# Which wait a reload leaves behind, and the order of two inverse mixings, in a gated convolution and MLP kernel

## The chip, the cores and the metric

The kernel runs on one core of a Trainium2 chip. Its time is the device time of one execution in microseconds (us); a median of several executions is quoted. Five engines run their own instruction streams and meet through semaphores: TensorE (PE in the profile; matmuls), VectorE (DVE; elementwise work), ScalarE (ACT; here it empties PSUM), GpSimd (POOL; here it issues accumulating DMA transfers) and SyncE (SP; issues the other transfers). A ratio is the mean time of one kernel's fast runs over that of the kernel before in the same rounds on the same chip, so it is not quite the ratio of the medians that stand beside it. Brackets after a ratio are its 95% interval.

## The reference, cut to what matters

```python
g = sigmoid((q * gate_w).sum(-1, keepdims=True))
kv = shift_conv4(k) * v                               # S = 2048 rows, D = 640 columns
y  = irfft(rfft(pad(kv)) * rfft(pad(ssm_k)))[:S]      # long convolution along S
a  = q * (y + kv * ssm_D)
b  = mlp_over_S(layernorm(q))                         # S -> 1536, gelu, -> S
return g * a + (1 - g) * b
```

The four-row phases p = 0..3 of the sequence are transformed as matmuls and combined by elementwise "mixing" steps, in both directions. The inverse is made in two halves of the output rows.

## The kernel before: the parts concerned

Every operation is handed to a small list scheduler in the program, which works out an order for each engine from dependencies and assumed durations, and then to a tracker, which emits the semaphore waits.

```python
# tracker: emits a DMA. "wait" is an extra region that must be complete first.
def dma(self, stream, out_ap, in_ap, semname, ..., wait=()):
    reads = [in_ap] + ([out_ap] if accum else []) + list(wait)   # recorded as read by the DMA
    acc = self.pre(stream, reads, [out_ap])                      # waits
    ...
    for reg, mode in acc:
        self.add_record(reg, mode, ("dma", semname, v))          # later writers wait for this DMA
# scheduler side of the same helper
    rd = [i] + ([o] if accum else []) + list(kw.get("wait", ()))

def invmix(Ya, Yb, sc, z0, z2):    # eight VectorE steps of 128 x 2560
    S0 = a0 + a1;  a0 = a0 - a1    # m1, m2
    S1 = b0 + b1;  b0 = b0 - b1    # m3, m4 (m4 overwrites b0)
    a1 = S0 + S1;  b1 = S0 - S1    # m5 -> inverse tile p=0, m6 -> p=2
    oA = ...;      oB = ...        # m7 -> p=1, m8 -> p=3
# ... (written out from the tensor_tensor calls)

chained(product, A0[1], ...)       # last spectral product with an accumulating DMA: C1 += SS ("C<-SS")
for kt in range(2):                # q_hi is scratch until that sum is done; now reload it with q
    dma(q_hi[:, kt], q_from_HBM, 128 * 5120, wait=[H(A0[1], 1)])
chained(product, A0[0], ...)
for kt in range(2):
    dma(q_lo[:, kt], q_from_HBM, 128 * 5120).after.add(w2last)
Z0 = invmix(A0[0], A0[1], C3a, None, None);      inverse(0, Z0)   # m1..m8
Z1 = invmix(A1[0], A1[1], (SS, 0), None, None);  inverse(1, Z1)   # n1..n8
```

m1 to m8 are the first half's steps, n1 to n8 the second half's. For each tile p, 16 matmuls make the inverse, ScalarE scales two results into cgb, and VectorE multiplies by q ("q product").

Of the kernel before, what the change touches and what calls it, by code (L numbers as in the profile page):

```python
# [13 lines left out]
ALU = mybir.AluOpType  # L14
# [4 lines left out]
class _Tracker:  # L19
# [231 lines left out]
        self.dma_cnt[name] = 0  # L251

    def dma(self, stream, out_ap, in_ap, semname, transpose=False, noncontig=False, accum=False, wait=()):
        reads = [in_ap] + ([out_ap] if accum else []) + list(wait)
        writes = [out_ap]
        acc = self.pre(stream, reads, writes)
        engobj = self.eng[stream]
        sem = self.dma_sems[semname]
        if transpose:
            ins = engobj.dma_start_transpose(out_ap, in_ap)  # L260
        elif accum:
            ins = engobj.dma_start(out_ap, in_ap, accum_op=ALU.add, max_dma_last_dim=2560)  # L262
        elif noncontig:
            with self.nc.allow_non_contiguous_dma(reason="tiny"):
                ins = engobj.dma_start(out_ap, in_ap)
        else:
            ins = engobj.dma_start(out_ap, in_ap)
        ins.then_inc(sem, 16)
        self.dma_cnt[semname] += 16
        v = self.dma_cnt[semname]  # L270
        self.dma_hist[(semname, v)] = dict(self.known[stream])
        src = ("dma", semname, v)
        for reg, mode in acc:
            self.add_record(reg, mode, src)
        return v
# [234 lines left out]
def _build(nc, A_q, A_k, A_v, A_shift_k, A_ssm_k, A_ssm_D, B_x, B_w1, B_b1, B_w2, B_b2, gate_w, out):  # L510
    Bsz, S, D = A_q.shape
# [9 lines left out]
    with ExitStack() as es:  # L521
# [8 lines left out]
        SC = _Sched(T, pp)  # L530
# [4 lines left out]
        def alloc(name, shape, dtype, at=None):  # L535
            size = mybir.dt.size(dtype)
            for s_ in shape[1:]:
                size *= s_
            if at is None:
                off = cur[0]  # L540
                cur[0] = (off + size + 63) // 64 * 64
            else:
                off = at
            assert off % 4 == 0 and off + size <= top, f"SBUF overflow {name}: {off}+{size} > {top}"
            h = nc.alloc_sbuf_tensor_at(name, list(shape), dtype, offset=off)
            T.reg_sbuf(h, off)
            return h

        def base_of(h):
            return T.mem[h.name][1]  # L550

        def V(h, off, dims, p0=0, pn=128):
            row = T.mem[h.name][2]
            return bass.AP(tensor=h, offset=p0 * row + off, ap=[[row, pn]] + [list(d) for d in dims])
# [26 lines left out]
        SS = alloc("SS", [128, 2, 4, D], BF16)  # L581
# [22 lines left out]
        q_hi = alloc("q_hi", [128, 2, 4, D], BF16, at=base_of(Drow))  # L604
# [3 lines left out]
        def n_of(ap):  # L608
            n = 1
            for st, ct in [tuple(p) for p in ap.ap][1:]:  # L610
                n *= ct
            return n

        def dve_dur(n, mode):
            return n / {1: 960.0, 2: 1920.0, 4: 3840.0}[mode] + (0.04 if mode == 4 else 0.08)
# [4 lines left out]
        def tt(eng, o, a, b, op, mode=2, prio=None, xr=()):  # L620
            n = n_of(o)
            d = dve_dur(n, mode) if eng == "DVE" else n / 600.0 + 0.17
            rd = [a, b] + list(xr)
            o_ = SC.add(eng, d, lambda s: T.op(eng, lambda e: e.tensor_tensor(o, a, b, op), rd, [o]),  # L624
                        rd, [o], prio=prio, name="tt")
            o_.lock = True
            return o_
# [23 lines left out]
        def act(o, i, func, bias=None, scale=None, acc=None, vt=None, prio=None, name="act"):  # L651
            kw = {}
            rr = []
            nap = 0
            for k_, v_ in (("bias", bias), ("scale", scale)):
                if v_ is not None:
                    kw[k_] = v_
                    if isinstance(v_, bass.AP):
                        rr.append(v_)
                        nap += 1  # L660
            ww = [o]
            if acc is not None:
                kw["accum_out"] = acc
                ww.append(acc)

            def emit(s):
                src = i(s) if vt is not None else i
                return T.op("ACT", lambda e: e.activation(o, src, func, **kw), rr + [src], ww)  # L668
            return SC.add("ACT", act_dur(n_of(o), nap), emit, rr if vt is not None else rr + [i], ww, prio=prio, vt=vt, name=name)
# [31 lines left out]
        def dma(o, i, nbytes, stream="SP", prio=None, sem=None, rate=365.0, chain=False, **kw):  # L701
            if sem is None:
                sem = f"d{ndma[0]}"
                ndma[0] += 1
            if sem not in T.dma_sems:
                T.add_dma_sem(sem, es.enter_context(nc.semaphore(f"s_{sem}")))
            rd = [i] + ([o] if kw.get("accum") else []) + list(kw.get("wait", ()))
            o_ = SC.add(stream, nbytes / rate / 1000.0, lambda s: T.dma({"QA": "ACT"}.get(stream, stream), o, i, sem, **kw), rd, [o], prio=prio, lat=-1.0, name="dma")
            if chain:
                if last[0] is not None:  # L710
                    o_.after.add(last[0])
                last[0] = o_
            return o_

        def dr(t, off, ap):
            return bass.AP(tensor=t.tensor, offset=t.offset + off, ap=ap)
# [383 lines left out]
        for n_, hk in enumerate(HORD):  # L1100
            for a in range(3):
                w2last = dma(W2[:, W2S[n_][a]:W2S[n_][a] + 4, :], dr(B_w2, a * 4 * 128 * S + 512 * hk, [[S, 128], [128 * S, 4], [1, 512]]), 128 * 4096)
            for p in range(4):
# [13 lines left out]
                if not last_:  # L1117
                    o_ = act(O1[:, hk, p, :].rearrange("p (a b) -> p a b", a=2), two, ACT.Identity, bias=c2[:, t:t + 1], scale=omg[:, t:t + 1], vt=vt, name="o1")

        A0 = {0: (C[2], 2), 1: (C[1], 0)}  # L1120
        A1 = {0: (C[3], 2), 1: (C[3], 0)}
# [9 lines left out]
        def H(hs, c):  # L1131
            h, s = hs
            return V(h, s * SL + 1280 * c, [[SL, 2], [1, 1280]])
# [24 lines left out]
        C3a = (C[2], 0)  # L1158

        def acc_dma(dst, src):  # L1160
            (hd, sd), (hs, ss) = dst, src
            for i in range(2):
                o = V(hd, (sd + i) * SL, [[1280, 2], [1, 1280]])
                i_ = V(hs, (ss + i) * SL, [[1280, 2], [1, 1280]])
                dma(o, i_, 128 * 5120, stream="POOL", prio=0, accum=True)
# [22 lines left out]
                dma(comp(V1[g], i, 0), tmp, 128 * 5120, stream="POOL", prio=0, accum=True)  # L1188


        def invmix(Ya, Yb, sc, z0, z2):
            def sl(h, s):
                return V(h, s * SL, [[1, SL]])

            def pr(h, s, rev=False):
                return V(h, s * SL + (1280 if rev else 0), [[-1280 if rev else 1280, 2], [1, 1280]])
            (ha, sa), (hb, sb), (hs, ss) = Ya, Yb, sc
            tt("DVE", sl(hs, ss), sl(ha, sa), sl(ha, sa + 1), ALU.add)
            tt("DVE", sl(ha, sa), sl(ha, sa), sl(ha, sa + 1), ALU.subtract)
            tt("DVE", sl(hs, ss + 1), sl(hb, sb), sl(hb, sb + 1), ALU.add)  # L1200
            tt("DVE", sl(hb, sb), sl(hb, sb), sl(hb, sb + 1), ALU.subtract)
            tt("DVE", sl(ha, sa + 1), sl(hs, ss), sl(hs, ss + 1), ALU.add)
            tt("DVE", sl(hb, sb + 1), sl(hs, ss), sl(hs, ss + 1), ALU.subtract)
            oA = V(hs, ss * SL, [[SL + 1280, 2], [1, 1280]])
            oB = V(hs, (ss + 1) * SL, [[-1280, 2], [1, 1280]])
            tt("DVE", oA, pr(ha, sa), pr(hb, sb, True), ALU.add)
            tt("DVE", oB, pr(ha, sa), pr(hb, sb, True), ALU.subtract)
            return {0: (ha, sa + 1), 2: (hb, sb + 1), 1: (hs, ss), 3: (hs, ss + 1)}

        def inverse(h, Z):  # L1210
# [40 lines left out]
        def chained(f, *a):  # L1251
            n0 = len(SC.ops)
            f(*a)
            new = [o for o in SC.ops[n0:] if o.eng == "DVE"]
            for o in new:
                o.after.update(lastp[-1:])
            lastp.append(new[-1])
# [4 lines left out]
        acc_dma(A1[1], V1[1])  # L1262
        acc_dma(A1[0], V1[0])
        chained(product, A0[1], A0[1], V0[1], H(V0[1], 0))
        for kt in range(2):
            dma(q_hi[:, kt, :, :], dr(A_q, 512 * kt * D, [[4 * D, 128], [1, 4 * D]]), 128 * 5120, wait=[H(A0[1], 1)])
        chained(product, A0[0], A0[0], V0[0])
        for kt in range(2):
            dma(q_lo[:, kt, :, :], dr(A_q, (1024 + 512 * kt) * D, [[4 * D, 128], [1, 4 * D]]), 128 * 5120).after.add(w2last)
        Z0 = invmix(A0[0], A0[1], C3a, None, None)  # L1270
        inverse(0, Z0)
        Z1 = invmix(A1[0], A1[1], (SS, 0), None, None)
        inverse(1, Z1)

        SC.run()
# [35 lines left out]
```

## Time and profile before

| | before |
|---|---|
| first three executions | 183.45, 184.76, 185.66 us; median 184.76 |
| span of the profiled execution (first to last instruction) | 181.9 us |
| TensorE busy, VectorE busy | 173.2 us, 171.3 us |
| TensorE's idle time from 100 us to its last matmul | 1.74 us, one hole before 158.25 |

The span is what the profile shows; the device time is some 2 us more.

### The profile page before, as it was taken

The page shows a single profiled execution, that of the slowest core. Times are in us where ns is not written, and L with a number is a line of the kernel's source. Part 1 is how long each engine was busy: PE and PEld are TensorE (multiplying, and loading weights), DVE is VectorE, ACT ScalarE, POOL GpSimd, SP SyncE. Part 2 cuts the span into 40 slices and gives each one's busy share as a digit, 9 for nine tenths or more (in the row PEclk, how much of TensorE's full clock was granted, in tenths as well). Part 3 has the DMA queues.
Part 4 walks back from the last instruction along what each step waited for, and adds up shares of the span by engine and source line. Part 5 has one row for each costly group of instructions (what it writes and reads, how often), then busy time and mean ns, then how long its engine had stood idle before and what let it go on. Part 6 is the DMA issues. An engine that isn't in the chain of part 4 may idle for free.

```text
span 181.9 us, 3336 instructions
## 1 busy us (share of the span) xinstructions
PE 173.2 (95%) x1380; PEld 129.3 (71%) x1381; DVE 171.3 (94%) x203; ACT 116.9 (64%) x176; POOL 45.3 (25%) x42
## 2 busy tenths in 40 slices
PE   7969998899999999999999999999999999699993
PEld 2636785586778677776777778888888887477772
DVE  7999895999999999999999899999999996999974
ACT  5798998899898999428999911322313225156760
POOL 4089404580000055000241101205252000041300
PEclk9999999999999999999999999999999999999999
DMA  5999999999999999998499799797999999146787
GB/s 159 376 410 370 389 269 200 266 397 300 213 262 269 176 279 234 230 229 220 110 269 260 147 180 349 143 216 236 189 194 227 204 241 416 66 76 144 123 258 271
DMA packets 38542, 43.51 MB, mean 239 GB/s; under 512 B 15867, under 2 KB 31360, under 8 KB 38528
## 3 DMA queue, kind: packets, MB, share of 16 engines
q1 hardware_dynamic: 33296, 32.16, 58.0%
q0 software_dynamic: 5200, 11.14, 35.2%
q8 instruction: 11, 0.18, 0.4%
q14 instruction: 3, 0.02, 0.0%
q10 hardware_dynamic: 32, 0.01, 0.0%
HBM read 25.87 MB, written 2.62 MB: 157 GB/s over the span
## 4 chain that ended last, share of the span: by engine, by line
PE 47%; ACT 19%; DVE 18%; DMA 11%; issue 3%; SPq 0%; DVEq 0%
PE pp L293 47%; DVE C L624 10%; DMA C<-SS 5%; DMA q_hi<-in_A_q_dram 5%; ACT C L668 5%; ACT gq L668 5%; DVE tm L624 4%; ACT FTB L668 3%; ACT wT L668 3%; DVE q_hi L624 2%; ACT ksh L668 2%; ACT GT L668 2%; DVE SS L624 1%; ACT L668 1%; DVE O L680 0%
## 5 line engine op out<-in xcount | busy, mean ns | idle before, releaser
L293 PE MATMUL pp<-X,ring 128*128 128x320 bf16 x384 | 55.4, 299 | 0.0
L624 DVE TENSOR_TENSOR C<-C 128x2560 bf16<-128x2560 bf16 (+2 forms) x37 | 54.5, 1521 | 0.3 <-DMA q_hi<-in_A_q_dram 0.3
L293 PE MATMUL pp<-GT,W 128*128 128x320 bf16 x384 | 52.8, 299 | 0.0
L293 PEld LDWEIGHTS pp<-GT,W 128*128 128x128 bf16 x384 | 43.5, 113 | 8.7
L293 PEld LDWEIGHTS pp<-X,ring 128*128 128x128 bf16 x384 | 37.4, 98 | 14.4
L668 ACT ACTIVATE C<-pp 128x640 bf16<-128x640 f32 x64 | 40.4, 724 | 4.7 <-PE pp L293 4.7
L668 ACT ACTIVATE O<-pp,c,omg 128x640 bf16<-128x640 f32 x15 | 13.2, 883 | 33.8 <-PE pp L293 33.8
L262 POOL DMA_DIRECT2D C<-C x8 | 10.9, 1610 | 41.9 <-DVE C L624 38.4
L293 PE MATMUL pp<-wT,FTB 128*128 128x320 bf16 x112 | 17.2, 299 | 2.6 <-ACT wT L668 1.5
L668 ACT ACTIVATE cgb<-pp,gg 128x640 bf16<-128x640 f32 x16 | 12.7, 793 | 8.5 <-PE pp L293 8.5
L293 PEld LDWEIGHTS pp<-wT,FTB 128*128 128x128 bf16 x112 | 10.5, 98 | 7.9 <-ACT wT L668 2.0
L668 ACT ACTIVATE GT<-pp,cc 128x640 bf16<-128x640 f32 x12 | 9.5, 795 | 9.0 <-PE pp L293 9.0
L293 PE MATMUL pp<-C,FTB 128*128 128x320 bf16 x96 | 13.5, 299 | 1.7 <-DVE C L624 1.7
L624 DVE TENSOR_TENSOR tm<-C,C 128x2560 bf16<-128x2560 bf16 (+1 forms) x7 | 14.3, 2057 | 0.0
L920 DVE BATCH_NORM_STATS2 stats<-X 128x6 f32<-128x320 bf16 x32 | 13.5, 462 | 0.0
L293 PEld LDWEIGHTS pp<-C,FTB 128*128 128x128 bf16 x96 | 9.3, 98 | 5.6 <-issue 2.0
L624 DVE TENSOR_TENSOR SS<-C 128x2560 bf16<-128x2560 bf16 x8 | 11.8, 1486 | 1.3 <-DMA C<-C 1.3
L262 POOL DMA_DIRECT2D C<-q_hi x6 | 5.9, 977 | 27.7 <-DVE C L624 13.2
L262 POOL DMA_DIRECT2D O<-q_hi x4 | 4.8, 1200 | 28.5 <-DVE q_hi L624 28.5
L668 ACT ACTIVATE gq<-gq 128x640 bf16<-128x640 bf16 x16 | 11.8, 739 | 0.0
L624 DVE TENSOR_TENSOR C<-tm 128x2560 bf16<-128x2560 bf16 (+1 forms) x9 | 10.6, 1191 | 0.1
L668 ACT ACTIVATE wT<-pp 128x1024 bf16<-128x1024 f32 x10 | 9.7, 1043 | 1.0 <-PE pp L293 1.0
(73 smaller groups left out, 200.4 us busy)
## 6 DMA issues: line engine op xcount, KB each, us to landing
ring<-in_B_w_dram SPq DMA_DIRECT2D x12, 512.0 KB, 9.9
W<-in_B_w_dram SPq DMA_DIRECT2D x12, 512.0 KB, 6.3
C<-C POOLq DMA_DIRECT2D x8, 640.0 KB, 10.5
X<-in_A_q_dram SPq DMA_DIRECT2D x4, 640.0 KB, 8.4
kn<-in_A_k_dram SPq DMA_DIRECT2D x4, 640.0 KB, 9.1
out_dram<-O SPq DMA_DIRECT2D x7, 320.0 KB, 3.0
C<-SS POOLq DMA_DIRECT2D x3, 640.0 KB, 11.5
ssm<-in_A_ssm_k_dram SPq DMA_DIRECT2D x3, 512.0 KB, 6.8
```

Source lines behind the costliest of these rows:

```text
L262: ins = engobj.dma_start(out_ap, in_ap, accum_op=ALU.add, max_dma_last_dim=2560)
L293: ins = self.nc.tensor.matmul(ps_ap, lhsT=lhsT, rhs=rhs, start=start, stop=stop, skip_group_check=True)
L624: o_ = SC.add(eng, d, lambda s: T.op(eng, lambda e: e.tensor_tensor(o, a, b, op), rd, [o]), rd, [o], prio=prio, name="tt")
L668: return T.op("ACT", lambda e: e.activation(o, src, func, **kw), rr + [src], ww)
L920: ops.append(SC.add("DVE", 0.38, (lambda o, i: lambda s: T.op("DVE", lambda e: e.bn_stats(o, i), [i], [o]))(o, i), [i], [o]))
```

## The change

Its intent: the reload of q_hi has to wait for the last sum C<-SS, but nothing that overwrites C1 afterwards has to wait for the reload; and the second half's mixing shall not be put in front of the first half's, since the first half's tiles are needed first.

```diff
     def dma(self, stream, out_ap, in_ap, semname, ..., wait=()):
-        reads = [in_ap] + ([out_ap] if accum else []) + list(wait)
+        reads = [in_ap] + ([out_ap] if accum else [])
         writes = [out_ap]
+        if wait:
+            self.pre(stream, list(wait), [])
         acc = self.pre(stream, reads, writes)
...
-            rd = [i] + ([o] if kw.get("accum") else []) + list(kw.get("wait", ()))
+            rd = [i] + ([o] if kw.get("accum") else [])
...
+            for o_ in SC.ops[n0:]:          # at the end of invmix
+                o_.after.update(behind or ())
...
+        lastacc = SC.ops[-1]
...
-            dma(q_hi[...], ..., wait=[H(A0[1], 1)])
+            dma(q_hi[...], ..., wait=[H(A0[1], 1)]).deps.add(lastacc)
...
-        Z0 = invmix(A0[0], A0[1], C3a, None, None)
+        Z0 = invmix(A0[0], A0[1], C3a)
+        z0last = SC.ops[-1]
         inverse(0, Z0)
-        Z1 = invmix(A1[0], A1[1], (SS, 0), None, None)
+        Z1 = invmix(A1[0], A1[1], (SS, 0), False, [z0last])
```

(An option to start the mixing with b is added too and not used.) I call the first half of it, the record of the reload, part 1, and the order of n behind m part 2.

More of the change, by code (lines that the diff above doesn't have):

```diff
@@ L1188, in cross, with invmix @@
                 dma(comp(V1[g], i, 0), tmp, 128 * 5120, stream="POOL", prio=0, accum=True)
-        def invmix(Ya, Yb, sc, z0, z2):
+        def invmix(Ya, Yb, sc, bfirst=False, behind=None):
+            n0 = len(SC.ops)
             def sl(h, s):
@@ L1197, in invmix @@
             (ha, sa), (hb, sb), (hs, ss) = Ya, Yb, sc
-            tt("DVE", sl(hs, ss), sl(ha, sa), sl(ha, sa + 1), ALU.add)
-            tt("DVE", sl(ha, sa), sl(ha, sa), sl(ha, sa + 1), ALU.subtract)
-            tt("DVE", sl(hs, ss + 1), sl(hb, sb), sl(hb, sb + 1), ALU.add)
-            tt("DVE", sl(hb, sb), sl(hb, sb), sl(hb, sb + 1), ALU.subtract)
+            for (hy, sy), k in (((hb, sb), 1), ((ha, sa), 0)) if bfirst else (((ha, sa), 0), ((hb, sb), 1)):
+                tt("DVE", sl(hs, ss + k), sl(hy, sy), sl(hy, sy + 1), ALU.add)
+                tt("DVE", sl(hy, sy), sl(hy, sy), sl(hy, sy + 1), ALU.subtract)
             tt("DVE", sl(ha, sa + 1), sl(hs, ss), sl(hs, ss + 1), ALU.add)
@@ L1264, in _build @@
         chained(product, A0[1], A0[1], V0[1], H(V0[1], 0))
+        lastacc = SC.ops[-1]
+        assert lastacc.eng == "POOL"
         for kt in range(2):
-            dma(q_hi[:, kt, :, :], dr(A_q, 512 * kt * D, [[4 * D, 128], [1, 4 * D]]), 128 * 5120, wait=[H(A0[1], 1)])
+            dma(q_hi[:, kt, :, :], dr(A_q, 512 * kt * D, [[4 * D, 128], [1, 4 * D]]), 128 * 5120, wait=[H(A0[1], 1)]).deps.add(lastacc)
         chained(product, A0[0], A0[0], V0[0])
```

## The prediction

> **What bounds the kernel now.** I read the page first: TensorE is busy 173.2 us and VectorE 171.3 us of a span of 181.9, so two engines are nearly full and only a wait that ends in an empty TensorE can be worth anything. The chain of work that ended last, in order of time, says where such a wait may be. Its end in the kernel before:
>
> ```profile
> 133.98 9.76 DMA C<-SS
> ...
> 144.19 9.53 DMA q_hi<-in_A_q_dram
> ...
> 153.81 4.31 DVE C L624 x3
> 158.12 0.14 issue
> 158.25 20.82 PE pp L293 x152
> 179.08 0.02 issue
> 179.10 0.55 DVE O L680
> ```
>
> Columns are start, duration, engine or transfer, what it writes. Read upwards: the last 20.8 us are unbroken matmuls; they were released by three VectorE operations; those by the reload of q_hi from HBM (the diff's title says "key", the loads are of A_q); and that by the accumulating transfer C<-SS, the last addition to the second spectrum of the first half. A serial chain of two transfers, 133.98 to 153.72, stands in front of the inverse mixing.
>
> The chain overstates its worth: while the transfers ran, TensorE had other work. So I next read TensorE alone in order of time:
>
> ```profile
> 142.77 8.31 PE L293 MATMUL pp<-GT,W 128*128 128x320 bf16 x60
> 150.92 2.34 PE L293 MATMUL pp<-C,FTB 128*128 128x320 bf16 x16
> 153.10 3.42 PE L293 MATMUL pp<-GT,W 128*128 128x320 bf16 x24
> 158.25 2.33 PE L293 MATMUL pp<-C,FTB 128*128 128x320 bf16 x16 [1.74 <-DVE C L624]
> 160.43 2.34 PE L293 MATMUL pp<-GT,W 128*128 128x320 bf16 x16
> ```
>
> C,FTB is the inverse transform, GT,W the second matmul of the MLP, used as filler. There is one hole, 1.74 us before 158.25, and none elsewhere from 100 us on: the table of waits from there to the end has this as the only wait of TensorE. VectorE in the same stretch:
>
> ```profile
> 143.64 4.30 DVE L624 TENSOR_TENSOR C<-C 128x2560 bf16<-128x2560 bf16 x3
> 147.85 1.49 DVE L624 TENSOR_TENSOR SS<-C 128x2560 bf16<-128x2560 bf16 x1
> 149.25 1.48 DVE L624 TENSOR_TENSOR C<-C 128x2560 bf16<-128x2560 bf16 x1
> 152.01 1.49 DVE L624 TENSOR_TENSOR SS<-C 128x2560 bf16<-128x2560 bf16 x1 [1.28 <-DMA C<-C]
> 153.81 4.30 DVE L624 TENSOR_TENSOR C<-C 128x2560 bf16<-128x2560 bf16 x3 [0.30 <-DMA q_hi<-in_A_q_dram]
> 158.02 0.82 DVE L624 TENSOR_TENSOR q_hi<-cgb,q_hi 128x1280 bf16<-128x1280 bf16 x1
> ```
>
> Call the eight steps of the first half's inverse mixing m1 to m8, those of the second half n1 to n8 (in the order of the new source: add a, subtract a, add b, subtract b, then the four outputs 5, 6, 7, 8 that feed inverse tiles p = 0, 2, 1, 3). From the output names and the order in which the program's own scheduler issues the kernel before, the rows are m1, m3, m2; n3; m5; n1; m4, n2, m6; then the first q product. So m4 is the step held by q_hi, m6 comes two steps behind it, and p2 cannot run before m6 ends at 158.11. The n1 in front of m4 waited 1.28 us for the second half's last C<-C accumulation. The source explains m4: the reload records the "wait" region as read by the transfer itself, so m4, which overwrites C1[0], has a write-after-read wait on the reload's landing, though the reload reads HBM.
>
> **What the Trainium skill says.** "DMA: Bandwidth & Descriptors", section "Rules for kernel authors", says that an accumulating transfer must have signalled before another access of the same bytes; so the wait of the mixing on C<-SS is a true one and must stay. Here it landed at 143.74, and m3 needs it from 145.0: no cost left. Its section "Anatomy of one DMA" gives 2.0 us plus bytes over 436 GB/s, which would be an estimate of 3.5 us for a 640 KB reload; the trace has 9.53, since four reloads and the accumulations overlap, and the trace decides. "VectorE: DVE Perf Modes", section "The perf-mode tier table", caps tensor_tensor in bf16 at 2x: 2560 / 1.92 GHz = 1.33 us; the trace steps by 1.40 from start to start. "TensorE: Matmul & The Clock Gate", section "Wait — 56ns, not 53.3ns?", gives N / 2.4 GHz + 2.5 ns, 135.8 ns at 320 columns; the trace has 20.81 us for 152 matmuls, 136.9 ns, at granted clock 1.00. So no engine can go faster; only the hole can go.
>
> **The change, part by part.**
> Part 1, the reload's wait on the last sum only: the same wait is issued on the same queue, and the explicit dependency keeps its place in the schedule. The reload still starts at 143.8 and lands at about 153.7. Removed is m4's wait on it. No instruction is added or removed.
>
> Part 2, n1 to n8 behind m8: removed are the two second-half steps (n3, n1) in front of m4 and n2 in front of m6, and with n1 its 1.28 us wait, since C<-C has landed (152.0) long before n1 runs.
>
> I replay VectorE with 1.40 us a step of 2560, 0.74 for a q product, and 0.1 where a step needs the one before it. m1, m3, m2: 143.64 to 147.85 as now. m4 takes the place of n3: to 149.25. m5: to 150.65, as now, so p0 starts on TensorE at 150.92, as now. m6: to 152.05. m7: to 153.55. m8: to 154.97. q product p0 to 155.71: its q_hi landed at 153.7 and its p0 tile left PSUM at 154.09 (as in the trace, 153.30 + 0.79), so neither stops it. n1 to 157.1, q product p2 to 157.9, n2 to 159.3, q product p1 to 160.0, n3 to 161.4, q product p3 to 162.1, n4 to 163.5, n5 to about 165.0.
>
> TensorE: a tile p is 16 matmuls, 2.19 us. p0 150.92 to 153.11; p2 (needs m6, 152.05) to 155.30; p1 (m7, 153.55) to 157.49; p3 (m8, 154.97) to 159.68. The filler left is 24 + 16 = 40 matmuls, 5.48 us: to 165.16. Then n5 is due: 165.0 plus about 0.15 for the signal, so a gap of 0 to 0.1. The second half's 64 inverse matmuls take 8.76, the last 24 of the MLP 3.29: end at 177.2 to 177.3. Check by the sum: 192 matmuls from 150.92 are 26.28 us, 177.20. Before it was 179.06 to 179.08. The gain is 1.85 (the hole with its signal), less up to 0.1: about 1.75 us.
>
> VectorE agrees: after m5 it has 11 steps of 1.40 and 4 products of 0.74, 18.4 us, in both kernels. Before it took 150.73 to 170.78, 20.05 us, of which 1.28 + 0.30 were idle. The last n8 now ends near 169.2, and p3 of the second half needs it only at 171.7. The tail (last scale-and-add 0.55, store to 181.9) hangs on the last matmul as before and is unchanged. So 1.75 / 181.9 = 0.95%: the median 184.76 becomes 183.0.
>
> The change looks larger on the chain than it is: it takes about 10 us of transfer off it, and most of that goes to nothing because TensorE filled the time with MLP matmuls that must be done anyway.
>
> **Rivals.**
> 1. The hole moves rather than closes. Four first-half tiles now run back to back, and the filler that was spread between p0 and p1 must cover until n5. My replay leaves 0 to 0.1 us, with nothing in hand. If VectorE loses 1 us between 150 and 165 (say, the first q product waiting for a late q_hi: slack 154.97 - 153.72 = 1.25), the hole is back at p0 of the second half. That would give 183.9 to 184.8. For it: no margin. Against: every VectorE time in it is from this trace, and the C<-C wait is gone.
> 2. The scheduler, seeing the gap before n5, uses the last MLP tile (24 matmuls, kept in PSUM for the final additions) as filler. Then the kernel would end on an inverse tile and its tail: after TensorE's end, evacuation to +1.0 (as for p0), product 0.82, add 0.49, scalar 0.38, two scale-and-adds 1.2, about 3.9 instead of 0.55. At most some 3 us worse than my time: 185 to 186. Against: this tile has the lowest priority and 40 others stand before it; with the scheduler's own constants (1.0875 us per eight matmuls, 1.41 a step) my hand replay has n5 ready less than 0.1 us before the filler ends. Close, but it holds.
> 3. Nothing: the true wait is on C<-SS, and the reload was hidden anyway. Against: m4 shows the reload's landing as its releaser (0.30), and removing only that would move it by 0.30; but part 2 removes n3, n1 and n2 from in front too. That would be the size (some 0.3 us) if reordering failed: 184.5.
> 4. More than 1.75 us: the timed runs of before spread from 183.45 to 185.66, and its profiled run, at 183.71, lies low in them. If slower runs are those with a later landing of the reload, they carry a bigger hole, and the new kernel, with 1.25 us of slack, would save up to 1 us more: 182.
>
> **Range and chances.** The time is 183.0. The range 181.6 to 184.5 takes in rivals 3 and 4 at its ends and the spread of the runs (about 0.6% either way). Faster by over 2% needs 3.7 us, twice the only hole that exists: 0.03. Slower by over 2% needs rival 2 with bad luck on top: 0.02. Within 2%: 0.95.
>
> **What would show it.** Right: in the changed profile VectorE runs eight mixing steps of the first half without idle from 143.6 to about 155, the next step, SS<-C, has no wait on C<-C, TensorE shows four inverse tiles in a row (64 matmuls on C from 150.9), then 40 MLP matmuls, and no wait above 0.3 us; the last matmul ends near 177.3. The chain no longer contains q_hi. Wrong: a TensorE wait on SS or C near 165 (rival 1), GT,W matmuls not the last on TensorE (rival 2), or p0 starting later than 150.9 because C<-SS landed later.

## The result, and the profile after

The changed kernel took 181.81 us (median of 6; 181.63 to 182.82), the kernel before in the six executions by then 183.76; ratio 0.988 [0.9832, 0.9927]. That is faster by 1.2%, inside 2%. The chain that ended last, in order of time, in the changed kernel (start, duration, what):

```profile
37.59 3.29 ACT ksh L670 x4
40.89 0.05 issue
40.93 136.12 PE pp L295 x1048
177.06 0.02 issue
177.08 0.55 DVE O L682
```

The transfers have left the chain. From 40.93 us to the last scale-and-add it is one unbroken run of 1048 matmuls. TensorE in order of time:

```profile
150.68 8.86 PE L295 MATMUL pp<-C,FTB 128*128 128x320 bf16 x64
159.37 5.60 PE L295 MATMUL pp<-GT,W 128*128 128x320 bf16 x40
164.93 4.51 PE L295 MATMUL pp<-C,FTB 128*128 128x320 bf16 x32
169.27 4.51 PE L295 MATMUL pp<-SS,FTB 128*128 128x320 bf16 x32
173.62 3.42 PE L295 MATMUL pp<-GT,W 128*128 128x320 bf16 x24
```

The four inverse tiles of the first half stand together (64), the 40 filler matmuls behind them, and no line carries a wait in brackets. VectorE over the same stretch:

```profile
143.40 8.50 DVE L626 TENSOR_TENSOR C<-C 128x2560 bf16<-128x2560 bf16 x6
151.94 2.89 DVE L626 TENSOR_TENSOR C<-C,C 128x2560 bf16<-128x2560 bf16 x2
154.75 0.82 DVE L626 TENSOR_TENSOR q_hi<-cgb,q_hi 128x1280 bf16<-128x1280 bf16 x1
155.49 1.48 DVE L626 TENSOR_TENSOR SS<-C 128x2560 bf16<-128x2560 bf16 x1
```

m1 to m8 run without a break from 143.40, the first q product follows at 154.75, and n1 (SS<-C) finds its accumulation landed: no bracket either. VectorE's waits of 1.28 and 0.30 us are gone.

**Where the 2.2 us of span went.** The two profiles also differ before the change matters: p0 starts at 150.92 in one and at 150.68 in the other, although the instructions up to there are the same. From the start of p0 to the start of the two last scale-and-adds it is 178.43 - 150.92 = 27.51 us before and 176.41 - 150.68 = 25.73 after: 1.78 us is the hole. The other 0.24 is the start, and about 0.2 the last store. The experiments say which of this is real.

### The profile page after: what moved, and what is told of

It reads as the page before. It is cut to its first block, busy times and chain, and to the rows that moved or that the text cites. A ratio compares the mean times of both kernels' runs of the same rounds, so it can differ in the third digit from the quotient of the medians.

```text
span 179.7 us, 3335 instructions
## 1 busy us (share of the span) xinstructions
PE 173.1 (96%) x1381; PEld 128.7 (72%) x1381; DVE 171.2 (95%) x203; ACT 116.9 (65%) x176; POOL 43.7 (24%) x42
## 4 chain that ended last, share of the span: by engine, by line
PE 88%; ACT 10%; DVE 0%; issue 0%
PE pp L295 88%; ACT wT L670 3%; ACT C L670 2%; ACT ksh L670 2%; ACT FTB L670 2%; ACT L670 1%; ACT GT L670 0%; DVE O L682 0%; DVE zz L686 0%; ACT cw L670 0%; DVE cst L686 0%
## 5 line engine op out<-in xcount | busy, mean ns | idle before, releaser
L670 ACT ACTIVATE ksh<-pp 128x1024 bf16<-128x1024 f32 (+1 forms) x12 | 9.8, 894 | 0.6 <-PE pp L295 0.6
```

Of the source, the lines that this page charges most:

```text
L670: return T.op("ACT", lambda e: e.activation(o, src, func, **kw), rr + [src], ww)
```

## The experiments

Sixteen matmuls of a tile p take 2.2 us here; "hole" is idle TensorE in front of a tile. "Stretch" is the time from the start of p0 to the start of the last scale-and-adds, as above: it leaves out the scatter of the start and of the last store.

**control** has the new source with both parts undone; only the reload's explicit dependency on the last sum stays. In its trace TensorE and VectorE run the same groups in the same order as before's from 140 us on.

> The kernel before, written with the new source and both parts undone: the same instructions in the same order on every engine. Any theory: ratio to before 1.000 within 0.3%. It also gives a second profile of before: if its inverse matmuls start at 150.9 us again, the 0.24 us by which the changed kernel started them earlier belongs to the change; if they start anywhere in 150.6 to 151.2, it is scatter of the first loads.

It measured 183.87 us, ratio 0.9992 [0.9966, 1.0018]. In its profile p0 starts at 151.23, the hole is 1.88 us and the stretch 27.65. So starts scatter, and the 0.24 us does not belong to the change.

**after_again** is the changed kernel, without an edit.

> The changed kernel once more. Theory (the gain is the one hole of TensorE, 1.75 us, and the rest of the 2.2 us between the two profiles is scatter at the start and at the last store): 1.7 to 1.9 us less than before, ratio 0.990 to 0.991. Rival (slow executions of before have a larger hole, which the change also closes): 2.2 us or more less, ratio 0.988 or lower, and the profile of the control shows a hole above 2 us.

It measured 181.95 us, ratio 0.988 [0.9856, 0.9903]; p0 at 150.66, stretch 25.72. The ratio is the rival's, but the control's hole of 1.88 is not "above 2 us", so the rival isn't borne out either. The looks at before below settle that.

**p1_reload_only** keeps part 1 and undoes part 2:

```diff
-        Z1 = invmix(A1[0], A1[1], (SS, 0), False, [z0last])
+        Z1 = invmix(A1[0], A1[1], (SS, 0), False, None)
```

> Part 1 alone: the reload's wait on the last sum only; the second half's mixing may go between the first's. The schedule then puts only n1 in between, after m6. Theory A (the recorded read of the reload is the whole cause, since the scheduler saw that dependency too and filled m4's place with n3 and n1): n1 starts at 152.0, just when C<-C has landed, no hole on TensorE before p2, all of the gain: 1.7 us less than before, level with the changed kernel within 0.2%. Theory B (my prediction's rival 3: without part 2 the n steps stay in front of m4, and only 0.3 us is won): 183.4, ratio to before 0.998.

It measured 181.68 us, ratio 0.9879 [0.9855, 0.9902]: level with the changed kernel. VectorE in order of time:

```profile
144.26 8.50 DVE L626 TENSOR_TENSOR C<-C 128x2560 bf16<-128x2560 bf16 x6
152.68 1.48 DVE L626 TENSOR_TENSOR SS<-C 128x2560 bf16<-128x2560 bf16 x1
154.08 2.88 DVE L626 TENSOR_TENSOR C<-C,C 128x2560 bf16<-128x2560 bf16 x2
```

n1 alone stands in between, without a wait, and the stretch is 25.61, so part 2 on top of part 1 adds nothing (25.73 with it). Theory A holds, theory B falls: the scheduler had put n3 and n1 in front only because the recorded read told it that m4 must wait.

**p2_order_only** keeps part 2 and puts the recorded read back, in the tracker and in the scheduler:

```diff
-        reads = [in_ap] + ([out_ap] if accum else [])
+        reads = [in_ap] + ([out_ap] if accum else []) + list(wait)
-        if wait:
-            self.pre(stream, list(wait), [])
-            rd = [i] + ([o] if kw.get("accum") else [])
+            rd = [i] + ([o] if kw.get("accum") else []) + list(kw.get("wait", ()))
```

> Part 2 alone: the second half's mixing behind the first's, the reload still recorded as a reader of C1. Theory A: m5 is moved before m4, m4 waits for q_hi to about 153.8, m6 ends near 156.6, and nothing else may fill VectorE; TensorE has a hole of about 2.8 us before p2 and then uses half of the last MLP tile as filler: 0.9 us slower than before, ratio 1.005. Theory B (part 2 carries the gain by taking n3, n1 and n2 out of m4's and m6's way): at least 1 us faster than before.

It measured 186.62 us, ratio 1.0141 [1.0106, 1.0177], slower by 2.6 us where 0.9 was expected. TensorE in order of time:

```profile
149.84 2.34 PE L293 MATMUL pp<-C,FTB 128*128 128x320 bf16 x16
152.02 2.34 PE L293 MATMUL pp<-GT,W 128*128 128x320 bf16 x16
156.84 4.01 PE L293 MATMUL pp<-C,FTB 128*128 128x320 bf16 x16 [2.49 <-DVE C L624]
...
179.70 1.79 PE L293 MATMUL pp<-GT,W 128*128 128x320 bf16 x12
```

The hole is 2.49 us, near the 2.8 expected and 0.75 more than before's 1.74. Two costs come on top. After the hole 16 matmuls take 4.01 us instead of 2.34, 1.67 us more: the granted clock was 0.68 from 156.8 to 157.8, 0.50 from there to 160.0 and 0.72 in the microsecond after. And half of the last MLP tile had been used as filler, as expected, so that only 12 matmuls follow the last inverse tile; the end hangs on that tile's evacuation, product, addition and scale-and-adds, to 182.96 where the last matmul ended at 181.49, while in before the last scale-and-add ends some 0.57 after it: 0.9 us more. The parts 0.75 + 1.67 + 0.9 make 3.3, and the profiled span is 3.6 longer than before's (185.5 against 181.9); the other 0.3 stands after the last scale-and-add. Three of the six executions had clock 0.987 to 0.988 and spans of 185.2 to 185.6, three had 0.997 to 0.998 and 183.9 to 184.2: it seems that the throttle strikes only in some of them. The mean is between.

**wait_only** has the order of before on every engine, and only the emitted semaphore wait of m4 is gone (tracker changed, scheduler as before, no part 2).

> The order of before on every engine, with only the wait of m4 on the reload's landing gone. Theory A: m4 starts right after n1, 0.3 us earlier, the hole shrinks from 1.74 to about 1.45: 0.3 us less than before, ratio 0.998. Theory B (the wait itself is the cost, as the chain with its 9.5 us of reload suggests): most of 1.75 us.

It measured 183.94 us beside 184.38 for before, ratio 0.9978 [0.9915, 1.0041]; 0.3 us is below what these rounds tell. VectorE, then TensorE, in order of time:

```profile
152.49 1.49 DVE L626 TENSOR_TENSOR SS<-C 128x2560 bf16<-128x2560 bf16 x1 [1.25 <-DMA C<-C]
...
158.33 2.33 PE L295 MATMUL pp<-C,FTB 128*128 128x320 bf16 x16 [1.32 <-DVE C L626]
```

The hole is 1.32 us, in the place of 1.74 to 1.88: about 0.5 less. The wait itself is a small part; the order that the same record had caused keeps most of the hole, since n1 in front of m4 still waits 1.25 us for C<-C.

**order_with_wait** has the order of the changed kernel, with the recorded read kept in the tracker alone, so that m4 waits on the reload again.

> The order of the changed kernel on every engine, with the wait of m4 on the reload kept. m4 stands fourth on VectorE and holds all behind it from 147.85 to about 153.7; m5, and with it p0, come 5.8 us later, and TensorE has no filler in front: a hole of about 5.8 us at 150.9, 3.9 us slower than before, ratio 1.021. If the order alone were worth the gain, it would be faster than before.

It measured 190.03 us, ratio 1.0287 [1.0219, 1.0354], slower by 5.4 us on the means. The stretches of its trace (columns: the window in us, its length, then busy time of PE, PEld, DVE, ACT and POOL with instruction counts, granted clock, DMA share, GB/s):

```profile
151.00:157.20 6.20, 0.90 (x7) 0.49 (x5) 3.00 (x3) 0.74 (x1) 0.00 (x0) 0.92 0.85 349
157.20:160.00 2.80, 2.76 (x11) 1.64 (x12) 2.77 (x3) 0.43 (x1) 0.00 (x0) 0.50 0.00 0
160.00:162.00 2.00, 2.00 (x10) 1.07 (x9) 1.42 (x2) 0.66 (x2) 0.00 (x0) 0.50 0.00 0
162.00:164.00 2.00, 2.00 (x12) 1.31 (x11) 1.47 (x2) 0.94 (x2) 0.34 (x1) 0.73 0.04 8
164.00:166.00 2.00, 2.00 (x17) 1.43 (x15) 1.29 (x2) 1.42 (x3) 0.86 (x1) 1.00 0.33 52
```

The hole of 5.34 us is there, and for over 5 us after it TensorE ran at half clock: the 64 matmuls took 11.71 us where the changed kernel took 8.86, 2.85 more. So neither the order nor the wait can be judged by itself: with the wait, the new order is the worst kernel of all; without it, the old order keeps its hole.

**late_a** and **late_b** delay the reload in the changed kernel, to try how much slack the first q product has. PE, DVE, ACT and POOL keep their order; the reload is issued behind the first, or behind both, q_lo reloads:

```diff
         for kt in range(2):
             dma(q_lo[...], ...).after.add(w2last)
+        for o_ in reloads:                     # the two q_hi reloads
+            o_.after.update(SC.ops[-2:])       # late_a: SC.ops[-2:-1]
+            o_.dur = 0.01                      # only so that the scheduler keeps its order
```

> The changed kernel with the same order on PE, ACT, DVE and POOL, its q_hi reload issued behind the first q_lo reload, near 147 instead of 143.6. The first q product now runs at 154.75 and the reload lands 1.0 to 1.2 us before it. Theory: the landing moves to 155 to 157, the q product waits that excess, and TensorE shows a hole before p0 of the second half as long as that wait, plus 0.1: 0.5 to 2.5 us slower than the changed kernel. Rival (there is more slack than that): no difference.

late_a measured 182.2 us beside 184.38 for before, ratio 0.9858 [0.979, 0.9925]: no loss to be seen, in an interval too wide for one below about 1 us. p0 started 2.0 us later in this profile than in the changed kernel's (152.69), so its times must be shifted by that. The cause lies at the start, where a first load came late:

```profile
7.49 0.96 PE L295 MATMUL pp<-ident,ssm 128*128 128x128 bf16 x8 [1.53 <-DMA ssm<-in_A_ssm_k_dram]
```

After this hole of 1.53 us the granted clock was 0.50 from 8 to 11 us, and the mean of the execution is 0.991. The reload was issued 3.7 us later, and yet the q product ran on time (156.79, which is 154.78 in the changed kernel's time) without a wait: the median landing took 6.4 us in place of 8.5. An issue 3.7 us later thus did not mean a landing 3.7 us later; why is not shown.

> As late_a, with the q_hi reload behind both q_lo reloads, issued near 152. Theory: it lands near 158.5, the first q product waits about 3.7 us, the hole before p0 of the second half is about 3.8 us, 3.8 us slower than the changed kernel and 2 us slower than before (ratio to before 1.01). Rival (VectorE regains it from its idle time further back): less than 1 us slower than the changed kernel.

late_b measured 186.04 us, ratio 1.0072 [1.0002, 1.0141]. VectorE, then TensorE, in order of time:

```profile
157.84 0.82 DVE L626 TENSOR_TENSOR q_hi<-cgb,q_hi 128x1280 bf16<-128x1280 bf16 x1 [2.28 <-ACT cgb L670]
...
168.03 4.51 PE L295 MATMUL pp<-C,FTB 128*128 128x320 bf16 x32 [2.32 <-DVE C L626]
```

The q product waited 2.28 us. The profile names ScalarE, but the two scaled results of p0 were there by 154.59, so it must be the reload, issued from 151.03 and with up to 6.2 us to its landing. The hole in front of p0 of the second half is 2.32, as long as the wait. That is the prediction's first rival, made on purpose: VectorE has nothing in hand between m5 and n5. The stretch is 179.51 - 151.42 = 28.09, 2.4 us over the changed kernel's; the expected 3.8 was too much because the reload landed sooner than thought. The three executions not profiled have 183.9 to 185.1 us of span and clock 0.991. A lower clock after the hole would fit, but the profiled late_a has 0.991 from its start alone; where these three lost their time is not shown.

**before_look2, before_look3, before_look4** are three more looks at the instructions of before.

> The instructions of before once more, for a look at its hole. The timed gain pooled over two variants is 2.17 us, plus or minus 0.25, the hole in the two profiles of before 1.74 and 1.88. Theory A (the hole differs from execution to execution and is larger on average than in the first profile): among the three looks there is one of 2.0 or more. Theory B (the rest of the gain comes from elsewhere): all three looks lie at 1.7 to 1.9.

> Third look at the same program, with the same two theories as for the second look: one of the three at 2.0 us or more, or all at 1.7 to 1.9.

> Fourth look at the same program, with the same two theories as for the second look: one of the three at 2.0 us or more, or all at 1.7 to 1.9.

The holes are 1.86, 1.83 and 1.82 us, the stretches 27.62, 27.60 and 27.59: theory A falls. The third took 185.43 us against 183.62 and 183.55 for the others, with the same hole, granted clock 1.00. It lost its time at the start. Its TensorE in order of time:

```profile
8.03 0.71 PE L293 MATMUL pp<-ident,ssm 128*128 128x128 bf16 x8 [0.97 <-DMA ssm<-in_A_ssm_k_dram]
...
152.47 2.34 PE L293 MATMUL pp<-C,FTB 128*128 128x320 bf16 x16
...
159.89 2.33 PE L293 MATMUL pp<-C,FTB 128*128 128x320 bf16 x16 [1.82 <-DVE C L624]
```

A first load came late: the group that waits for it ran at 8.03, where before_look2 ran it at 6.00. Only 0.97 us of that shows as a wait, since TensorE was itself some 1 us behind by then (eight and then three matmuls in front took 1.07 and 1.48 us in place of 0.73 and 0.81). p0 started at 152.47 in place of 150.68 to 151.23.

**gap_closed** tries the one gap that was left in the changed kernel:

```diff
+        q3 = [o for o in SC.ops if o.eng == "DVE"][-1]    # q product of p3, first half
...
+        q3.after.add(SC.ops[n1 + 4])                      # behind n5
```

> The changed kernel with the first half's fourth q product moved behind n5, so that p0 of the second half is ready 0.7 us sooner. Theory: the only gap left, about 0.1 us before 164.9, closes and nothing else changes: 0 to 0.1 us, not to be told from the changed kernel by the clock (ratio to before 0.988); in the profile 192 matmuls from p0 to the end take 26.3 us, not 26.4. Rival (VectorE still bounds the end): 0.5 us or more.

It measured 181.77 us, ratio 0.9889 [0.9868, 0.991], beside 183.74 for before. Its stretch is 25.61 against 25.73 and 25.72: the 0.1 us is there in the profile, too little to be told in the times. It beats before and is level with the changed kernel; I know of no version here that beats both.

## Why the prediction was right or wrong, point by point

Two steps failed: the base from which the gain was taken off, and the share of the two parts in it. The path, TensorE's hole behind the held VectorE steps, was right, and the size of the gain nearly so.

**The bound and the hole: right.** The gain that the traces can place is the hole of TensorE, and most of the 10 us of transfers on the chain was worth nothing. VectorE's replay, step by step, holds to 0.1 us: m8 predicted to end at 154.97 from a start of 143.64, and the q product began at 154.75 from a start of 143.40, which is 154.99 on the same count. The 1.33 us and 135.8 ns that the prediction works out from the pages' figures are estimates; the traces' 1.40 us and 136.9 ns were used in the replay. (1.75 / 181.9 is 0.96%, not 0.95%; it changes nothing.)

**The first rival (no slack between m5 and n5): as described, and it did not happen.** TensorE lost about 0.1 us there. late_b shows the hole move there once the reload is late enough; in late_a, issued 3.7 us later, it did not.

**The second rival (last MLP tile as filler): did not happen in the changed kernel.** It happened in part in p2_order_only, at some 0.9 us.

**The size of the gain: nearly right, somewhat small.** The prediction took the hole with its signal from one look, 1.85 us, less up to 0.1: 1.75. The first pair of profiles has 1.78 on the stretch. But that look's hole, 1.74 us, is the smallest of five (1.74, 1.88, 1.86, 1.83, 1.82). On the stretch, before takes a mean of 27.59 us over its five looks and the changed kernel 25.73 over its two: 1.87. Two executions whose p0 started at the same 150.68, before_look2 and the first look after, took 183.62 and 181.63 us: 1.99. The timed gain, pooled over control with its before (17 executions) and after_again with p1_reload_only (11), is 2.17 us with an interval of about 0.25 either way. What stays open is whether the last 0.1 to 0.3 is more than scatter.

**The base: the term at which the number failed.** "The median 184.76 becomes 183.0" built on three executions, of which two were slow ones. In the later sessions before had medians of 183.94, 184.38 and 183.74. Of the 1.2 us between 183.0 and 181.81, about 1.0 is the base (184.76 against 183.76) and about 0.2 the gain. The prediction saw the spread and, in its fourth rival, read it the wrong way: slow runs were to have a larger hole. The one slow execution that was looked at, before_look4, has the same hole and a late start; the two slow ones of the first three were not profiled.

**Part 2: wrong.** The prediction said that the order, by taking n3, n1 and n2 away, carried most of the gain, and that without it some 0.3 us would be won. Alone, part 1 gave all of it (0.9879), and part 2 alone lost 1.4%; taking out only m4's wait, with the old order kept (wait_only), took 0.5 us off the hole. The step that failed is that it treated the record of the reload as a wait only. It was a dependency of the scheduler as well, and the n steps had been put in front of m4 because of it.

## What to carry to other kernels

A helper that expresses "wait for this region" as "reads this region" makes every later writer wait for the transfer; and where a scheduler uses the same record, it orders the work around that false dependency too, so that taking out the wait alone can leave most of the cost (here 1.32 of some 1.8 us of hole). Price a chain of transfers by the idle time that it leaves on the fullest engine, not by its length. Take the base from enough executions, and compare inside the trace from a point where both kernels are still the same.

## What the Trainium skill lacked or had wrong

- "TensorE: Matmul & The Clock Gate", section "What's actually happening", puts the fall to half clock at one idle window of about 3.4 us or more, and says that the window runs freely. Here shorter holes were enough in two profiled executions: after 2.49 us in p2_order_only the clock was 0.50 from 157.8 to 160.0, and after 1.53 us at the start of late_a it was 0.50 from 8 to 11 us. Holes of 1.32 to 1.88 us after p0 and one of 2.32 were followed by full clock, so the length of one hole does not decide it alone; what does is not shown. After a hole of 5.34 us the clock was 0.50 from 157.2 to 162, which agrees with the page's half.
- "DMA: Bandwidth & Descriptors", section "Anatomy of one DMA — SWDGE (gpsimd) path", has a fit for one DMA that GpSimd issues; no page says when a transfer lands that SyncE issues among others. Here the same 640 KB reload took a median of 8.5 us in the changed kernel, and 6.4 us in late_a, where it was issued 3.7 us later.
- No page says how much the landing of the first loads scatters a kernel's time: two looks at one program ran the group that waits for an early load at 6.00 and 8.03 us, and started p0 at 150.68 and 152.47.
